# LSH attention and a feed-forward block on one core: all 192 normalisations on POOL, and a schedule that holds the durations of a trace

## The chip, the core and the metric

The kernel runs on one core of a Trainium2 chip. A core has five engines with queues of their own: PE (TensorE, matrix products and transposes), DVE (VectorE), ACT (ScalarE), POOL (GpSimd) and SP (SyncE, which here only issues transfers). Each works through its instructions in the order in which they were written and waits on semaphores. The metric is the device time of one launch in microseconds.

## The reference

Attention in which a query sees only the keys of its own hash bucket, and a two-layer feed-forward block on what it gives. Batch 4, 8 heads, 768 rows, head size 64; model width 512, inner width 2048; float32, but for the two weight matrices, which come as doubles.

```python
q_bucket = sum(((q @ proj) > 0) * powers)          # 6 bits; k_bucket likewise
scores = where(q_bucket == k_bucket, (q @ k.T) / 8, -1e9)
scores = scores - max(scores); attn = exp(scores)
attn = attn / (sum(attn) + 1e-9)
x = (attn @ v)                                     # heads side by side: 3072 x 512
h = x @ w_in
out = (s * relu(h)**2 + b) @ w_out
```

A query whose bucket holds no key keeps the score -1e9 in every column, and its weights are all 1/768.

## The kernel before

The work is cut into 96 slots: a slot is 256 queries of one head of one batch (two tiles of 128 queries). In each slot:

- `weights(i, a, pr)`, once for each tile a: two groups of score products of 384 keys (L416 for batch 0, in float32; L418 and L419 afterwards, in split float32r), the row maximum on DVE (L426), the exponential with its row sum on ACT (L427), and on DVE four one-column instructions, `inverse` (L433 to L436), that give the row's factor `rz` and summand `u`. The last of the four, L436, multiplies a comparison of one column with another column. Then the tile is normalised in place: e times rz plus u. For the second tile (a = 1) that is one DVE instruction right behind the inverse (L440), for the first tile (a = 0) one POOL instruction of the same form (L444).
- `values(i, pr, pieces)`: the normalised tiles are transposed by PE (L470, four at a time, two of each tile, so each set needs both tiles), copied out of PSUM (L475, or L481 with the rest L482) and multiplied with the values (L489, or L491 and L492); the result goes to `xpb`, is split into a high and a low part (L508, L509) and written out.
- Between the slots `prep` splits q and k of a later head, hashes them and copies their parts together (L344 to L369); `decode` turns one of 32 weight tiles from doubles into two float32r parts, with ACT (L287, L288, L293), DVE (L289, L290) and POOL (L291, L299, for half of them L298); `moe` is the feed-forward block of 256 rows in eight steps (L545 to L547 into the inner layer, ACT L551 to L553 and POOL L554, L562 to L564 out of it), 96 steps in all.

The score banks 0 and 1 of PSUM are shared by all tiles (for the first seven slots, 6 and 7 too): the next tile's scores can be written only when the exponential has read them.

Nothing is issued in the order in which it is written. Each piece is put on a `Plan` with an engine, a cost in microseconds, the keys that it reads and writes, and a priority. `Plan.order` is a list scheduler: it runs the pieces against these costs (and `HOP`, what a result takes to another engine) and gives each engine's queue its order. No time of the plan reaches the chip, only the order. The costs come from the helpers `act`, `dve` and `pool`, as a slope and a constant or as a number at the place of the call:

```python
def act(n, fn, r, w, pr, more=0.0):
    plan.add(ACT, 0.095 + n / 1200.0 + more, fn, r, w, pr)
```

Weights of a slot have the priority 10 i - 8, values 10 i + 5, decoding 10 i + 15, steps of `moe` from 100000 on: they fill.

Of the kernel before, what the change touches and what calls it, by code (L numbers as in the profile page):

```python
# [14 lines left out]
AF = mybir.ActivationFunctionType  # L15
ALU = mybir.AluOpType
# [11 lines left out]
PE, DVE, ACT, POOL, SP = (mybir.EngineType.PE, mybir.EngineType.DVE, mybir.EngineType.Activation,  # L28
                          mybir.EngineType.Pool, mybir.EngineType.SP)
# [80 lines left out]
def lsh_attention_moe(ctx: ExitStack, tc, q, k, v, proj, w_in, w_out, s, b, out):  # L110
    nc = tc.nc
    B, H, S, D = q.shape
# [4 lines left out]
    HS = S // 2  # L117
    CH = 256
# [15 lines left out]
    plan = Plan()  # L134

    def f32(ap):
        return ap.bitcast(F32)

    def tile_(name, shape, dt=F32):
        return const.tile(shape, dt, name=name)  # L140
# [5 lines left out]
    def pe(cost, fn, r, w, pr):  # L146
        plan.add(PE, cost, fn, r, w, pr)

    def dve(n, fn, r, w, pr, ns=None):
        plan.add(DVE, ((n + 64) / 960.0 if ns is None else ns), fn, r, w, pr)  # L150

    def act(n, fn, r, w, pr, more=0.0):
        plan.add(ACT, 0.095 + n / 1200.0 + more, fn, r, w, pr)

    def pool(n, fn, r, w, pr, ns=None):
        plan.add(POOL, (0.15 + n / 430.0 if ns is None else ns), fn, r, w, pr)
# [29 lines left out]
    xsb = tile_("xsb", [P, 2, CH], F32R)  # L186
# [6 lines left out]
    st = tile_("st", [P, NST, 4])  # L193
    thr, big, s_sb, b_sb, qk_sb = [misc[:, x:x + 1] for x in range(5)]
# [114 lines left out]
    def AK(x, r=(0, 1), g=(0, 1)):  # L309
        return [("aq", x, i, j) for i in r for j in g]  # L310

    def BK(x, r=(0, 1), g=(0, 1)):
        return [("bq", x, i, j) for i in r for j in g]
# [18 lines left out]
    def prep(w, i, pr):  # L332

        x, y, h, exact = visits[w]["x"], w % 2, visits[w]["h"], w < EARLY
        aq, bq, ks, nat = EQ[h] if exact else AQ[y], BQ[y], KS[y], NAT[y]
        mk, NK = nat.rearrange("p t j d -> p (t j d)"), [("nat", y, 0), ("nat", y, 1)]

        def split(g, i, pr):
            pb = fill_bank(i)
            cols, o = slice(g * HS, (g + 1) * HS), bank[:, pb, 0:HS]  # L340

            def tr():
                for t in range(HT):
                    nc.tensor.transpose(out=bank[:, pb, t * P:(t + 1) * P], in_=nat[:, g * HT + t], identity=ident)  # L344
            pe(0.33, tr, NK, [("b", pb)], pr)
            act(HS, lambda: nc.scalar.activation(aq[:, cols], o, AF.Copy, scale=qk_sb), [("b", pb)], AK(x, g=(g,)), pr)
            if exact:
                if g:
                    dma(lambda: EK[h][0:D, 0:S], lambda: aq[D:P, 0:S], AK(x, r=(1,)), [("ks", x, 0)], pr, D * S * 4)
                return  # L350
            dve(HS, lambda: nc.vector.scalar_tensor_tensor(bq[:, cols], o, qk_sb, f32(aq[:, cols]), ALU.mult, ALU.subtract), [("b", pb)] + AK(x, g=(g,)), BK(x, g=(g,)), pr, 0.55)
            if g:
                dma(lambda: ks[0:D], lambda: aq[D:P].rearrange("p (o n) -> p o n", o=1).broadcast_to([D, 2, S]), AK(x, r=(1,)), [("ks", x, 0)], pr, 2 * D * S * 4)
                dma(lambda: ks[D:P, 0], lambda: bq[D:P], BK(x, r=(1,)), [("ks", x, 1)], pr, D * S * 4)

        def hash_(g, i, pr):
            pb = fill_bank(i)
            cols, o = slice(g * HS, (g + 1) * HS), bank[:, pb, 0:HS]

            def mm():  # L360
                if exact:
                    nc.tensor.matmul(o[0:D], pj, aq[:, cols], start=True, stop=True)
                    return
                nc.tensor.matmul(o[0:D], pjh, aq[:, cols], start=True, stop=False)
                nc.tensor.matmul(o[0:D], pjl, aq[:, cols], start=False, stop=False)
                nc.tensor.matmul(o[0:D], pjh, bq[:, cols], start=False, stop=True)
            pe(mmc(HS, 4 if exact else 3), mm, AK(x, g=(g,)) + ([] if exact else BK(x, g=(g,))), [("b", pb)], pr)

            dve(HS, lambda: nc.vector.tensor_scalar(mk[0:KB + MR, cols], o[0:KB + MR], thr[0:KB + MR], big[0:KB + MR], ALU.is_gt, ALU.mult),  # L369
                [("b", pb)], NK, pr, 0.67)  # L370
            if g and exact:
                dma(lambda: EK[h][D:HR, 0:S], lambda: mk[KB:KB + MR], NK, [("ks", x, 2)], pr, MR * S * 4)
                dma(lambda: aq[D:HR, 0:S], lambda: mk[0:MR], NK, AK(x, r=(1,)), pr, MR * S * 4)
            elif g:
                dma(lambda: aq[D:P], lambda: aq[0:D], AK(x, r=(0,)), AK(x, r=(1,)), pr, D * S * 4)
                dma(lambda: ks[D:HR, 1], lambda: mk[KB:KB + MR], NK, [("ks", x, 2)], pr, MR * S * 4)
                dma(lambda: bq[D:HR], lambda: mk[0:MR], NK, BK(x, r=(1,)), pr, MR * S * 4)
            if g:
                n = preps.index(w) + 2
                if n < len(preps):  # L380
                    load(preps[n], pr)
        return [lambda i, pr, f=f, g=g: f(g, i, pr) for f in (split, hash_) for g in range(2)]
# [20 lines left out]
    def weights(i, a, pr):  # L403

        bb, h, c, w = slots[i]
        x, t, j, exact = visits[w]["x"], c * TPC + a, TPC * i + a, bb == 0
        b0 = 6 if i < EARLY - 1 and j % 2 else 0
        bk = [("b", b0), ("b", b0 + 1)]
        aq, bq, ks = AQ[w % 2], BQ[w % 2], KS[w % 2]
        ts = slice(t * P, (t + 1) * P)  # L410

        for g in range(2):
            def mm(g=g):
                cols, o = slice(g * HS, (g + 1) * HS), bank[:, b0 + g, 0:HS]
                if exact:
                    nc.tensor.matmul(o, EQ[h][0:HR, ts], EK[h][0:HR, cols], start=True, stop=True)  # L416
                    return
                nc.tensor.matmul(o, aq[:, ts], ks[:, 0, cols], start=True, stop=False)  # L418
                nc.tensor.matmul(o, bq[0:HR, ts], ks[0:HR, 1, cols], start=False, stop=True)  # L419
            pe(mmc(HS, 4 if exact else 2), mm, AK(x) + KK(x) + ([] if exact else BK(x)), [bk[g]], pr)  # L420
        y = j % NST
        nm, z, rz, u = [st[:, y, m:m + 1] for m in range(4)]
        e, ek = eb[:, j % NE], ("e", j % NE)

        sc = bank[:, b0:b0 + 2, 0:HS]
        dve(S, lambda: nc.vector.tensor_reduce(nm, sc, AX.XY, ALU.max, negate=True), bk, [("st", y, 0)], pr, 0.95)  # L426
        act(S, lambda: nc.scalar.activation(e.rearrange("p (g n) -> p g n", g=2), sc, AF.Exp, bias=nm, accum_out=z),  # L427
            bk + [("st", y, 0)], [ek, ("st", y, 1)], pr, 0.45)

        def inverse():
            nc.vector.tensor_scalar(rz, z, EPS, None, ALU.add)  # L433
            nc.vector.tensor_scalar(u, nm, -FLOOR, 1.0 / (S + EPS), ALU.is_gt, ALU.mult)
            nc.vector.reciprocal(rz, rz)
            nc.vector.scalar_tensor_tensor(rz, nm, -FLOOR, rz, ALU.is_le, ALU.mult)  # L436
        if a or i < DV:
            def norm():
                inverse()
                nc.vector.tensor_scalar(e, e, rz, u, ALU.mult, ALU.add)  # L440
            dve(S, norm, [("st", y, 0), ("st", y, 1)], [ek, ("st", y, 2)], pr, 1.37)
        else:
            dve(1, inverse, [("st", y, 0), ("st", y, 1)], [("st", y, 2)], pr, 0.65)
            pool(S, lambda: nc.gpsimd.tensor_scalar(e, e, rz, u, ALU.mult, ALU.add), [("st", y, 2)], [ek], pr, 2.23)  # L444

    xp, xd = {}, {}
    nx = [0]
# [1 line left out]
    def values(i, pr, pieces):  # L449


        bb, h, c, w = slots[i]

        vs, exact = VS[w % 2], i < EARLY
        x = visits[w]["x"] if exact else w % 2
# [5 lines left out]
        for f in range(HT):  # L461
            tb, y = fill_bank(i), nfill[1] % NPH
# [37 lines left out]
        t, tk = xp[key]  # L500
        xh, xk = t[hh * D:(hh + 1) * D], [tk + (hh,)]
# [3 lines left out]
        if hh:  # L505

            xk = [tk + (0,), tk + (1,)]
            act(CH, lambda: nc.scalar.copy(xsb[:, 0, :], t), xk, [("xs", 0)], pr)  # L508
            dve(CH, lambda: nc.vector.tensor_tensor(xsb[:, 1, :], t, f32(xsb[:, 0, :]), ALU.subtract), xk + [("xs", 0)], [("xs", 1)], pr)  # L509
            xd[key] = tc.dram_tile([P, 2, CH], F32R, name=f"xd{key[0]}_{key[1]}_{key[2]}")  # L510
            dma(lambda: xd[key], lambda: xsb, [("xs", 0), ("xs", 1)], [("xd", key)], pr, 262144)

# [77 lines left out]
    for i in range(NSL):  # L590
        pr = 10.0 * i
        bb, h, c, w = slots[i]
# [29 lines left out]
FIRST = 2.0  # L622
RATE = 1.6
PACE = 4
DV = 0
WP = -8
MP = 0.0
PP = 0
# [26 lines left out]
```

## Time and profile before

| what | value |
|---|---|
| median of 3 runs | 1154.06 us (1150.02 to 1154.14) |
| profiled execution, its own time | 1155.39 us |
| its span, first to last instruction | 1153.6 us |
| mean granted clock of TensorE | 0.964 |
| normalisations on DVE (L440) | 96, mean 815 ns |
| normalisations on POOL (L444) | 96, mean 1009 ns |

A line such as "L440 DVE TENSOR_SCALAR eb<-eb,st 128x768 ... x96" is a group: source line, engine, operation, what is written from what, shape, count. Behind the bar stand the busy time in us, the mean of one in ns, and the idle time of the engine just before these instructions with what ended it. A wait "PE bank L470 <- DVE eb L440: 11.2, 11, 2.5" reads: PE's instruction of L470 waited for DVE's of L440, 11.2 us in total, 11 times, the longest 2.5 us. The clock is the share of full speed that TensorE was granted.

### The profile page before, as it was taken

The numbers are of one execution on the slowest core, as the hardware profiler recorded it, in microseconds if no ns is written. First come the engines' busy times: TensorE is split into PE (matmuls) and PEld (weight loads), VectorE is DVE, ScalarE is ACT, GpSimd is POOL, SyncE is SP. The second block draws the span as 40 slices with busy tenths as digits, with TensorE's granted clock in tenths as the row PEclk, the third lists the DMA queues.
The fourth block names the chain that finished last, engine by engine and source line by source line (L and its number), as shares of the span: only waits on it lengthen the run. The fifth ranks groups of instructions, "written<-read, shape, count | busy, mean of one in ns | idle before, by whom it ended". The sixth has DMA issues, their size and how long they took to land.

```text
span 1153.6 us, 18828 instructions
## 1 busy us (share of the span) xinstructions
PE 1093.0 (95%) x6898; PEld 956.9 (83%) x6898; DVE 730.2 (63%) x1682; ACT 649.3 (56%) x1297; POOL 361.6 (31%) x318
## 2 busy tenths in 40 slices
PE   5987799988799999999999999999999999999998
PEld 2444487766699999989999999999999999999997
DVE  2666779868787878777777788778788860000000
ACT  2655476746566665756656666666666553333332
POOL 1465546635332222222222222222222222222221
PEclk7888899969899999999999999999999999999999
DMA  7463121213423342243243224324233201011010
GB/s 187 140 181 105 49 69 48 100 46 101 124 62 87 72 127 61 70 120 80 58 114 88 60 79 121 81 51 134 65 79 83 68 24 60 7 49 56 1 37 19
DMA packets 87980, 91.14 MB, mean 79 GB/s; under 512 B 55888, under 2 KB 61008, under 8 KB 87888
## 3 DMA queue, kind: packets, MB, share of 16 engines
q1 hardware_dynamic: 82976, 73.16, 23.7%
q10 hardware_dynamic: 4912, 16.78, 4.8%
q8 instruction: 54, 0.88, 0.3%
q14 instruction: 38, 0.31, 0.1%
HBM read 48.24 MB, written 18.87 MB: 58 GB/s over the span
## 4 chain that ended last, share of the span: by engine, by line
PE 86%; DVE 7%; DMA 2%; ACT 2%; issue 2%; SPq 0%; POOLq 0%; ACTq 0%; DVEq 0%
PE bank L470 10%; PE bank L545 8%; PE bank L546 8%; PE bank L547 8%; PE bank L564 7%; PE bank L563 7%; PE bank L562 7%; PE bank L492 5%; PE bank L491 5%; PE bank L416 5%; PE bank L419 4%; PE bank L418 4%; PE bank L489 2%; PE bank L344 2%; DVE eb L440 1%
## 5 line engine op out<-in xcount | busy, mean ns | idle before, releaser
L481 ACT CAST phdt.float32r<-bank 128x512 fp32r<-128x512 f32 x264 | 153.3, 585 | 177.0 <-PE bank L470 157.0
L426 DVE TENSOR_REDUCE st<-bank 128x1 f32<-128x768 f32 x192 | 183.3, 955 | 78.5 <-PE bank L416 39.6
L545 PE MATMUL bank<-xc,w 128*128 128x256 f32 x768 | 227.6, 296 | 0.0
L554 POOL TENSOR_TENSOR glb<-rb,ghb 128x512 fp32r<-128x512 f32 x96 | 124.8, 1300 | 317.1 <-ACT ghb L553 227.8
L546 PE MATMUL bank<-xc,w 128*128 128x256 f32 x768 | 217.9, 284 | 1.1 <-POOL w L299 1.1
L547 PE MATMUL bank<-xc,w 128*128 128x256 f32 x768 | 217.7, 283 | 0.0
L427 ACT ACTIVATE eb<-bank,st 128x768 f32<-128x768 f32 x192 | 173.6, 904 | 67.3 <-DVE st L426 66.1
L482 DVE TENSOR_TENSOR plb<-bank,phdt.float32r 128x512 fp32r<-128x512 f32 x264 | 178.4, 685 | 45.9 <-ACT phdt.float32r L481 44.2
L444 POOL TENSOR_SCALAR eb<-eb,st 128x768 f32<-128x768 f32 x96 | 96.9, 1009 | 334.7 <-DVE st L436 144.6
L470 PE MATMUL bank<-ident,eb 128*128 128x128 f32 x1152 | 180.0, 282 | 15.0 <-DVE eb L440 14.3
L470 PEld LDWEIGHTS bank<-ident,eb 128*128 128x128 f32 x1152 | 140.5, 145 | 37.7 <-DVE eb L440 16.3
L562 PE MATMUL bank<-w,ghb 128*128 128x512 f32 x384 | 156.9, 409 | 0.0
L564 PE MATMUL bank<-w,glb 128*128 128x512 f32 x384 | 152.2, 396 | 0.2 <-POOL glb L554 0.2
L563 PE MATMUL bank<-w,ghb 128*128 128x512 f32 x384 | 151.5, 395 | 0.0
L546 PEld LDWEIGHTS bank<-xc,w 128*128 128x128 f32 x768 | 147.1, 192 | 5.1 <-POOL w L299 1.6
L545 PEld LDWEIGHTS bank<-xc,w 128*128 128x128 f32 x768 | 147.0, 191 | 4.8 <-issue 0.7
L491 PE MATMUL bank<-phdt.float32r,vs 128*128 128x256 f32 x528 | 149.0, 304 | 1.6 <-ACT phdt.float32r L481 1.6
L547 PEld LDWEIGHTS bank<-xc,w 128*128 128x128 f32 x768 | 147.0, 191 | 0.0
L492 PE MATMUL bank<-plb,vs 128*128 128x256 f32 x528 | 139.8, 287 | 2.0 <-DVE plb L482 1.5
L551 ACT ACTIVATE rb<-bank 128x512 f32<-128x512 f32 x96 | 57.4, 598 | 147.7 <-PE bank L547 147.2
L570 DVE SCALAR_TENSOR_TENSOR osb<-bank,misc,bcs 128x512 f32<-128x512 f32 x24 | 17.4, 746 | 193.4 <-PE bank L564 193.2
L492 PEld LDWEIGHTS bank<-plb,vs 128*128 128x128 f32 x528 | 101.4, 192 | 9.9 <-DVE plb L482 4.3
(77 smaller groups left out, 1832.9 us busy)
## 6 DMA issues: line engine op xcount, KB each, us to landing
xd<-xsb SPq DMA_DIRECT2D x48, 256.0 KB
xc<-xd SPq DMA_DIRECT2D x48, 256.0 KB
ks<-aq SPq DMA_DIRECT2D x24, 384.0 KB
raw<-in_moe_w_in_dram ACTq DMA_DIRECT2D x16, 512.0 KB
raw<-in_moe_w_out_dram ACTq DMA_DIRECT2D x16, 512.0 KB
nat<-in_q_dram SPq DMA_DIRECT2D x32, 192.0 KB
nat<-in_k_dram SPq DMA_DIRECT2D x32, 192.0 KB
out_dram<-osb SPq DMA_DIRECT2D x24, 256.0 KB
```

The lines of the kernel that those rows point to most:

```text
L426: dve(S, lambda: nc.vector.tensor_reduce(nm, sc, AX.XY, ALU.max, negate=True), bk, [("st", y, 0)], pr, 0.95)
L427: act(S, lambda: nc.scalar.activation(e.rearrange("p (g n) -> p g n", g=2), sc, AF.Exp, bias=nm, accum_out=z), bk + [("st", y, 0)], [ek, ( ...
L470: nc.tensor.transpose(out=bank[:, tb, o:o + P], in_=eb[:, es[a], kt * P:(kt + 1) * P], identity=ident)
L482: dve(512, lambda ph=ph, pl=pl, src=src: nc.vector.tensor_tensor(pl, src, f32(ph()), ALU.subtract), [("b", tb), ("ph", y)], [("pl", y)], p ...
L491: nc.tensor.matmul(av, vs[:, kt], PH[0][:, y, m], start=(kt == 0), stop=False)
L492: nc.tensor.matmul(av, vs[:, kt], plb[:, y, m], start=False, stop=(kt == NT - 1))
L545: nc.tensor.matmul(hp, w[:, 0, fs], xc[:, 0, :], start=(cc == 0), stop=False)
L546: nc.tensor.matmul(hp, w[:, 1, fs], xc[:, 0, :], start=False, stop=False)
L547: nc.tensor.matmul(hp, w[:, 0, fs], xc[:, 1, :], start=False, stop=(cc == NC_ - 1))
L562: nc.tensor.matmul(o, gh[:, ts], w[:, 0], start=(f == 0), stop=False)
L563: nc.tensor.matmul(o, gh[:, ts], w[:, 1], start=False, stop=False)
L564: nc.tensor.matmul(o, gl[:, ts], w[:, 0], start=False, stop=(f == NF - 1))
```

## The change

Both tiles of a slot are normalised on POOL; DVE does the inverse alone. The constant `DV`, which was 0, goes. And costs of the plan are replaced: POOL's normalisation 1.01 us (2.23), the inverse 0.70 (0.65 alone, 1.37 together with DVE's normalisation), ACT's slope 1050 elements a microsecond (1200), the constant of the exponential 0.28 (0.45), of the scaled copy in `prep` 0.12 (none), its rest on DVE 0.61 (0.55), and the low part of x 0.5 (the slope gave 0.33).

```diff
     def act(n, fn, r, w, pr, more=0.0):
-        plan.add(ACT, 0.095 + n / 1200.0 + more, fn, r, w, pr)
+        plan.add(ACT, 0.095 + n / 1050.0 + more, fn, r, w, pr)
...
-            act(HS, lambda: nc.scalar.activation(aq[:, cols], o, AF.Copy, scale=qk_sb), [("b", pb)], AK(x, g=(g,)), pr)
+            act(HS, lambda: nc.scalar.activation(aq[:, cols], o, AF.Copy, scale=qk_sb), [("b", pb)], AK(x, g=(g,)), pr, 0.12)
...
         act(S, lambda: nc.scalar.activation(e.rearrange("p (g n) -> p g n", g=2), sc, AF.Exp, bias=nm, accum_out=z),
-            bk + [("st", y, 0)], [ek, ("st", y, 1)], pr, 0.45)
+            bk + [("st", y, 0)], [ek, ("st", y, 1)], pr, 0.28)
...
-        if a or i < DV:
-            def norm():
-                inverse()
-                nc.vector.tensor_scalar(e, e, rz, u, ALU.mult, ALU.add)
-            dve(S, norm, [("st", y, 0), ("st", y, 1)], [ek, ("st", y, 2)], pr, 1.37)
-        else:
-            dve(1, inverse, [("st", y, 0), ("st", y, 1)], [("st", y, 2)], pr, 0.65)
-            pool(S, lambda: nc.gpsimd.tensor_scalar(e, e, rz, u, ALU.mult, ALU.add), [("st", y, 2)], [ek], pr, 2.23)
+        dve(1, inverse, [("st", y, 0), ("st", y, 1)], [("st", y, 2)], pr, 0.70)
+        pool(S, lambda: nc.gpsimd.tensor_scalar(e, e, rz, u, ALU.mult, ALU.add), [("st", y, 2)], [ek], pr, 1.01)
...
-            dve(CH, lambda: nc.vector.tensor_tensor(xsb[:, 1, :], t, f32(xsb[:, 0, :]), ALU.subtract), xk + [("xs", 0)], [("xs", 1)], pr)
+            dve(CH, lambda: nc.vector.tensor_tensor(xsb[:, 1, :], t, f32(xsb[:, 0, :]), ALU.subtract), xk + [("xs", 0)], [("xs", 1)], pr, 0.5)
```

The text is six lines shorter behind the edit: L444 is L438 in the changed kernel, L470 is L464, L545 is L539, L554 is L548; up to L436 the numbers stay.

In the order, POOL's queue around the decoding of the fifteenth weight tile (raw_200 is that tile as it was read, w_... the tile decoded, bcs the column sums). Before:

```order
L444 TENSOR_SCALAR eb<-eb,st 128x768
L299 TENSOR_TENSOR w_809<-osb,w_809 128x512
L291 TENSOR_TENSOR osb<-osb,raw_200 128x512
L298 TENSOR_TENSOR bcs<-bcs,osb 128x512
L299 TENSOR_TENSOR w_846<-osb,w_846 128x512
L444 TENSOR_SCALAR eb<-eb,st 128x768
```

and now:

```order
L438 TENSOR_SCALAR eb<-eb,st 128x768
L299 TENSOR_TENSOR w_808<-osb,w_808 128x512
L291 TENSOR_TENSOR osb<-osb,raw_200 128x512
L438 TENSOR_SCALAR eb<-eb,st 128x768
L299 TENSOR_TENSOR w_834<-osb,w_834 128x512
```

A second normalisation stands between L291 and L299 of this tile, and the sum L298 has moved behind them.

The same place on DVE, which makes raw_200's bits (L289, L290) and then the inverse of a second tile. Before:

```order
L290 SCALAR_TENSOR_TENSOR osb<-osb,raw_200 128x512
L433 TENSOR_SCALAR st<-st 128x1
L434 TENSOR_SCALAR st<-st 128x1
L435 RECIPROCAL st<-st 128x1
L436 SCALAR_TENSOR_TENSOR st<-st 128x1
L440 TENSOR_SCALAR eb<-eb,st 128x768
L426 TENSOR_REDUCE st<-bank 128x1
```

and now:

```order
L290 SCALAR_TENSOR_TENSOR osb<-osb,raw_200 128x512
L433 TENSOR_SCALAR st<-st 128x1
L434 TENSOR_SCALAR st<-st 128x1
L435 RECIPROCAL st<-st 128x1
L436 SCALAR_TENSOR_TENSOR st<-st 128x1
L289 TENSOR_SCALAR raw_201<-osb 128x512
L426 TENSOR_REDUCE st<-bank 128x1
```

The normalisation is gone, and a part of the next tile's decoding stands in its place ahead of the next maximum.

More of the change, by code (lines that the diff above doesn't have):

```diff
@@ L350, in split @@
                 return
-            dve(HS, lambda: nc.vector.scalar_tensor_tensor(bq[:, cols], o, qk_sb, f32(aq[:, cols]), ALU.mult, ALU.subtract), [("b", pb)] + AK(x, g=(g,)), BK(x, g=(g,)), pr, 0.55)
+            dve(HS, lambda: nc.vector.scalar_tensor_tensor(bq[:, cols], o, qk_sb, f32(aq[:, cols]), ALU.mult, ALU.subtract), [("b", pb)] + AK(x, g=(g,)), BK(x, g=(g,)), pr, 0.61)
             if g:
@@ L624 @@
 PACE = 4
-DV = 0
 WP = -8
```

## The prediction

> **What bounds the kernel now.** I read the page first (shares and the 40 slices), then the busy times by stage, then what TensorE waited for in each stage, then the groups, the chain and the timeline of the one stage in which it waits.
>
> ```profile
> span 1153.6 us, 18828 instructions
> ...
> PE 1093.0 (95%) x6898; PEld 956.9 (83%) x6898; DVE 730.2 (63%) x1682; ACT 649.3 (56%) x1297; POOL 361.6 (31%) x318
> ...
> PE   5987799988799999999999999999999999999998
> ...
> DVE  2666779868787878777777788778788860000000
> ...
> PEclk7888899969899999999999999999999999999999
> ```
>
> TensorE (PE) is busy for 95% of the span, and the slices say where the other 5% lies: in the first eleven of the forty. The same stretch has the lowered clock. The busy times of four stretches make that exact (columns: stretch, its length, then PE, weight load, DVE, ACT and POOL busy with their counts, PE's granted clock, DMA share, GB/s):
>
> ```profile
> 0.00:120.00 120.00, 92.89 (x319) 50.12 (x319) 66.18 (x153) 61.10 (x119) 53.43 (x51) 0.83 0.56 149
> 120.00:325.00 205.00, 176.98 (x948) 140.49 (x947) 164.81 (x334) 125.18 (x258) 104.11 (x90) 0.90 0.25 76
> 325.00:925.00 600.00, 598.71 (x4199) 562.76 (x4198) 476.10 (x1148) 383.50 (x789) 153.03 (x138) 1.00 0.32 84
> 925.00:1153.60 228.60, 224.46 (x1438) 203.51 (x1436) 23.09 (x47) 79.55 (x135) 50.99 (x40) 1.00 0.09 32
> ```
>
> PE is idle for 27.1 us, 28.0 us, 1.3 us and 4.1 us of them. From 325 us on it is full at clock 1.00, so what DVE or POOL do there is hidden as long as they deliver in time. Only the first 325 us can get shorter. What PE waited for there, first 0 to 120 us, then 120 to 325 us (total, times, longest):
>
> ```profile
> PE bank L416 <- DMA eq<-in_v_dram: 7.2, 1, 7.2
> PE bank L344 <- DMA nat<-in_k_dram: 7.1, 2, 5.5
> PE bank L416 <- DMA eq<-nat: 3.3, 1, 3.3
> ```
>
> ```profile
> PE bank L470 <- DVE eb L440: 11.2, 11, 2.5
> PE bank L416 <- ACT eb L427: 8.2, 6, 1.7
> PE bank L364 <- DVE nat L369: 1.6, 1, 1.6
> ```
>
> The first 120 us wait on transfers, 17.6 us in these three rows, which the change does not touch. In the second stretch PE waits for two things: 11 times for the normalisation of a slot's second tile (L440, on DVE), and 6 times for an exponential (L427) to give back the score banks. The change moves the first; the second hangs on DVE's maximum (L426). The groups of that stretch (count, then busy us, mean ns, idle before):
>
> ```profile
> L440 DVE TENSOR_SCALAR eb<-eb,st 128x768 f32<-128x768 f32 x19 | 20.7, 1090 | 0.7
> L444 POOL TENSOR_SCALAR eb<-eb,st 128x768 f32<-128x768 f32 x20 | 20.7, 1034 | 56.7 <-DVE st L436 39.9 <-PE bank L470 10.8 <-PE bank L547 5.8
> L436 DVE SCALAR_TENSOR_TENSOR st<-st 128x1 f32<-128x1 f32 x38 | 18.7, 491 | 1.3
> L291 POOL TENSOR_TENSOR osb<-osb,raw 128x512 int32<-128x512 int32 x18 | 23.3, 1293 | 24.4 <-ACT eb L427 9.8 <-PE bank L492 4.2 <-DVE st L433 3.5
> ```
>
> The same normalisation takes 1.09 us on DVE and 1.03 us on POOL here. A timeline piece shows why DVE is so slow (start, duration, engine, line):
>
> ```profile
> 118.27 0.15 DVE L433 TENSOR_SCALAR st<-st 128x1 f32<-128x1 f32 x1 [1.13 <-ACT eb L427]
> 118.51 1.28 POOL L298 TENSOR_TENSOR bcs<-bcs,osb 128x512 f32<-128x512 f32 x1
> 118.65 1.15 DVE L436 SCALAR_TENSOR_TENSOR st<-st 128x1 f32<-128x1 f32 x1
> 119.98 0.98 POOL L444 TENSOR_SCALAR eb<-eb,st 128x768 f32<-128x768 f32 x1 [0.19 <-DVE st L436]
> ...
> 122.29 1.56 PE L416 MATMUL bank<-ek,eq 76*128 76x384 f32 x4 [1.72 <-ACT eb L427]
> 123.33 1.28 POOL L291 TENSOR_TENSOR osb<-osb,raw 128x512 int32<-128x512 int32 x1 [1.15 <-ACT osb L287]
> 123.50 1.13 DVE L436 SCALAR_TENSOR_TENSOR st<-st 128x1 f32<-128x1 f32 x1
> 124.67 1.70 DVE L440 TENSOR_SCALAR eb<-eb,st 128x768 f32<-128x768 f32 x1
> 124.69 1.26 POOL L298 TENSOR_TENSOR bcs<-bcs,osb 128x512 f32<-128x512 f32 x1
> 126.29 0.94 DVE L426 TENSOR_REDUCE st<-bank 128x1 f32<-128x768 f32 x1
> 126.42 1.33 PE L470 MATMUL bank<-ident,eb 128*128 128x128 f32 x5 [2.47 <-DVE eb L440]
> ```
>
> L436 works on one element per partition, yet it ends when POOL's instruction ends: 119.80 against 119.79 us, then 124.63 against 124.61 us. L440, behind it, is held by the next one (L298 to 125.95) and ends at 126.37. So one slot pays twice: PE stands 2.47 us, and the next maximum, whose scores were ready at 123.85 (122.29 + 1.56), starts 2.44 us late.
>
> **The change part by part.** All 96 of L440 leave DVE, 20.7 of its 164.8 busy us in the stretch that counts. POOL gets 19 more there; at 0.98 us it goes from 104.1 to 122.7 busy of 205 us (51% to 60%). The sum is of PE's idle time in that stretch.
>
> (a) Maxima no longer wait behind L440. What this is worth is the row of exponentials late for PE: between 0 and -8.2 us. The piece above has 1.70 of 2.44 us in L440, near the full end; in the new order a part of the decoding (L289) stands between L436 and the maximum at that place, which keeps some of it. I take -6.
>
> (b) The path from the inverse (end of L436) to PE's transposes. Before: 0.04 + 1.09 + 0.05 = 1.18 us (gaps from 124.63 to 124.67 and 126.37 to 126.42). After: 0.18 (119.80 to 119.98) + 0.98 + POOL to PE. The last gap I take from POOL's other client:
>
> ```profile
> 261.50 1.26 POOL L299 TENSOR_TENSOR w<-osb,w 128x512 fp32r<-128x512 f32 x1
> 262.82 0.39 PE L546 MATMUL bank<-xc,w 128*128 128x256 f32 x1 [1.12 <-POOL w L299]
> ```
>
> 0.06 us, so 1.22 us if POOL is free: +0.04 in each of 11 waits, +0.4 us in all. If each time a decoding instruction of 1.29 us goes first, 2.51 us: +14.6 us. In POOL's new order the normalisation stands right behind the L291 whose end releases L436, so it can start at once at that place; I take a fifth of the way, +3.
>
> (c) L436 meets POOL more often: its excess is 18.7 - 38 x 0.16 = 12.6 us; with POOL at 60% instead of 51% it is 14.9, +2.3 on DVE. The chain of that stretch holds it at 5.8% of 205 us, 11.9 of its 18.7 us, so about two thirds count: +1.5 (ends 0 and +2.3).
>
> ```profile
> by line: PE bank L416 14.1%; PE bank L470 10.1%; issue 5.9%; DVE st L436 5.8%; DVE eb L440 5.6%; PE bank L492 5.2%; DVE osb L290 5.0%; DVE st L426 4.2%; PE bank L491 3.9%; DVE plb L482 3.8%; ACT eb L427 3.1%; ACT phdt.float32r L481 2.6%; DM
> ```
>
> (d) L290, DVE's part of a weight's decoding, is 5.0% of the chain, 10.3 us, since the inverse queues behind it. With 20.7 of 164.8 us (13%) off the queue it comes earlier; I take a quarter, -2.5 (ends 0 and -4).
>
> (e) The cost table (ACT's slope, the exponential, L351 and L509) does no work of its own; it moves the order. MoE steps placed ahead of the 24th slot are 7.8 before and 7.9 after, the last slot has 59.6 and 60.6 of 96 ahead of it, so PE's work before and after 325 us is the same: 0. SP's queue has 360 rows in both; two pairs of loads (q and k of the sixth and the eighth head) go behind one or two copies. PE's waits for such loads are in the first stretch, 7.1 us in 2; I take 0, ends -3 and +3.
>
> Sum of idle: -6 + 3 + 1.5 - 2.5 = -4 us. The clock adds to that: at 0.90 the 177 us of work in the stretch are 17.7 us longer than at 1.00, beside 28 us of idle, 0.63 us for each idle us. That makes -6.5 us. The profiled execution took 1155.4 us (1.8 around the span), 1.3 above the median of the runs: 1148.9 against it, 1147.5 against the median.
>
> What hides the rest: from 325 us on POOL goes from 153 to 219 of 600 us (67 x 0.98 more), and 67 slots now hand their second tile to POOL. The cover is that PE has other work there. The plan allows 0.70 + 0.13 + 1.01 + 0.10 = 1.94 us from the inverse's start to the transposes; the rows give 0.54 (118.27 to the start of L436, and 0.16) + 0.18 + 0.98 + 0.06 = 1.76. If that cover goes, the rival below has its price.
>
> ```profile
> L436 DVE SCALAR_TENSOR_TENSOR st<-st 128x1 f32<-128x1 f32 x135 | 22.3, 165 | 4.6
> L444 POOL TENSOR_SCALAR eb<-eb,st 128x768 f32<-128x768 f32 x67 | 67.4, 1005 | 238.7 <-DVE st L436 77.1 <-PE bank L492 54.2 <-ACT aq L346 28.1
> ```
>
> These are L436 and POOL's normalisation from 325 to 925 us. L436 runs at 165 ns though POOL is busy a quarter of the time: POOL starts its long instructions right behind L436 or behind an ACT result, and the next L436 comes only after another exponential.
>
> **The rivals.** *POOL's queue makes it slower.* POOL works in order and carries the decoding. If the normalisation waits w behind it in each of the 11 cases, the idle changes by 11 x (0.04 + w) - 6 + 1.5 - 2.5; it breaks even at w = 0.60 us, and at a whole L291 (1.29) it is +7.6, with the clock +12.4: 1166.5 us. For: POOL is busy 60% of the stretch. Against: the held L436 means that POOL comes free at that very moment. Chance 0.15.
>
> *The relief changes nothing.* The bank loop (scores, maximum, exponential) goes on without the normalisation, and (a) and (d) are taken up by other DVE work that stood behind L440; then (b) and (c) cancel what is left: 1154 us. For: ACT's L427 waits are 6, L440's 11. Chance 0.25.
>
> *The full stretch loses its cover.* If L436 is held there as it is before 325 us, by (491 - 160) ns at a POOL share of 51%, then at the new share of 36% it is about 0.24 us late, and if PE waits for it in each of 67 slots, that is +16 us: 1163.5 us. Against: the 165 ns above, and PE's 1.3 us of idle in 600. Chance 0.08. The Trainium skill (GPSIMD Engine Reference, 1. Specifications) says that GpSimd shares its SBUF interfaces with VectorE and lists as contention VectorE's instructions with two SBUF inputs or in a 2-port mode. By that rule alone L436, which reads two SBUF columns, would be held wherever POOL works, and 1163.5 us would be the forecast; the trace bears it out at 491 ns up to 325 us and not at 165 ns after.
>
> *The change does not do what it says:* ruled out; no DVE instruction of that shape is left in the new order, and POOL has 192.
>
> **How the numbers follow.** The gain of some microseconds is likeliest: 1147.5 us, its own range 1139 to 1153 (from (a) at its end with (b) at +0.4, to half of (a)), chance 0.52. Half a per cent is 5.8 us, about what a measurement can tell from no change (the three runs spread over 4.1 us): below 1148.3 is faster. Of the 0.52, 0.45 lies below that and 0.07 above. Faster 0.45, the same 0.07 + 0.25 = 0.32, slower 0.15 + 0.08 = 0.23. The range leaves out the slower part of the slower cases, and below it reaches most of the way to (a) and (d) at their ends with the clock (-8.2 + 0.4 + 1.5 - 4 = -10.3, times 1.63: 1137.3): 1137 to 1161.
>
> **What would show it.** Right: in 120 to 325 us PE's idle falls from 28 to about 24 us and the clock rises a little; waits of L416 for L427 fall to 2 or 3 us; PE waits for L438 on POOL some 11 to 14 us in all; L436 rises to 0.55 us there and stays near 0.17 after; 325 to 925 us stays under 5 us idle. Wrong: PE's waits for POOL over 20 us, decoding ahead of L438 on POOL, L436 above 0.3 us after 325 us, or a change in the first 120 us, where the order moves but no row prices it.

## The result, and the profile after

The changed kernel takes 1160.86 us (median of 9 runs, 1156.63 to 1165.70) against 1152.28 us (9 runs, 1149.79 to 1155.22) for the kernel before on the same chip: a ratio of 1.0074, 95% interval 1.0052 to 1.0096. It is slower by 0.7%, where faster by 0.6% was forecast. The profiled execution took 1156.63 us, the shortest of its nine, while the profiled execution of before (1155.39 us) lay above the longest of its nine: the two traces stand closer to each other than the medians. The page of the changed kernel (span, engines, the slices of PE and its clock):

```profile
span 1154.8 us, 19001 instructions
...
PE 1090.9 (94%) x6898; PEld 954.7 (83%) x6898; DVE 659.6 (57%) x1586; ACT 650.0 (56%) x1297; POOL 453.8 (39%) x414
...
PE   5877799978899999989999999999999999999998
...
PEclk7789899988799999999999999999999999999999
```

The work has moved as planned: DVE 730.2 to 659.6 us, POOL 361.6 to 453.8. PE's weak slices are still the first eleven. The same stretches as before (length, then PE, weight load, DVE, ACT, POOL busy with counts, granted clock, DMA share, GB/s):

```profile
0.00:120.00 120.00, 85.51 (x281) 45.17 (x281) 59.77 (x138) 57.13 (x110) 53.29 (x52) 0.83 0.51 141
120.00:325.00 205.00, 184.61 (x1008) 145.81 (x1009) 151.89 (x330) 130.74 (x270) 130.59 (x116) 0.92 0.26 81
325.00:925.00 600.00, 595.04 (x4159) 558.44 (x4158) 420.68 (x1060) 379.62 (x778) 216.12 (x204) 1.00 0.32 84
```

From 120 to 325 us PE's idle time falls from 28.0 to 20.4 us, more than the 4 us forecast. But the first 120 us go from 27.1 to 34.5 idle, and hold 281 of PE's instructions instead of 319: the program is behind when the stretch ends. And 325 to 925 us go from 1.3 to 5.0. A stretch that ends at a fixed time mixes a delay with what it displaces, so from here on the stretches end at events of the trace: the start at the first maximum of the eighth slot, decoding where PE multiplies the finished column sums of the weights (L304, 8 to 12 us behind the last weight tile). Before, then after, the start and the decoding stretch:

```profile
0.00:116.20 116.20, 89.09 (x301) 47.66 (x302) 63.74 (x149) 58.27 (x113) 49.91 (x48) 0.82 0.58 154
116.20:328.60 212.40, 184.38 (x991) 146.39 (x991) 170.31 (x347) 129.95 (x267) 107.64 (x93) 0.90 0.24 74
```

```profile
0.00:124.80 124.80, 89.41 (x301) 47.55 (x302) 63.14 (x141) 58.91 (x113) 58.01 (x55) 0.84 0.51 141
124.80:326.00 201.20, 181.71 (x999) 144.42 (x999) 148.94 (x327) 129.95 (x268) 125.87 (x113) 0.92 0.25 79
```

The same 301 instructions of PE fill the start. It is 8.6 us longer, with 35.4 us of idle instead of 27.1: +8.3. The decoding stretch is 11.2 us shorter, with 19.5 instead of 28.0: -8.5. The two cancel, and what is lost in the full stretch (+3.7) stays.

What PE waited for in the start, the two rows that grew most (before, then after; "issue" is idle time for which the view finds no releaser):

```profile
PE bank L344 <- DMA nat<-in_k_dram: 7.1, 2, 5.5
PE bank L416 <- issue: 2.4, 1, 2.4
```

```profile
PE bank L344 <- DMA nat<-in_k_dram: 9.3, 3, 5.1
PE bank L416 <- issue: 9.2, 4, 3.5
```

Most of the +8.3 us is the second row, waits of score products (L416). The four begin 3.7 to 5.9 us after the issue of their own head's last copy, so that copy is likely what they wait for.

What PE waited for in the changed kernel, 120 to 325 us (total, times, longest):

```profile
PE bank L486 <- DVE plb L476: 6.8, 10, 1.4
PE bank L464 <- POOL eb L438: 6.4, 4, 2.9
PE bank L416 <- ACT eb L427: 3.0, 3, 1.7
PE bank L418 <- ACT eb L427: 2.5, 2, 1.4
```

and from 325 to 925 us:

```profile
PE bank L486 <- DVE plb L476: 3.0, 5, 1.2
PE bank L344 <- DVE bq L351: 1.2, 1, 1.2
PE bank L464 <- POOL eb L438: 0.3, 1, 0.3
```

The normalisation on POOL stops PE 4 times for 6.4 us (on DVE it was 11 times, 11.2 us). The banks cost 5.5 us (8.2). New is the wait of the value products for the low part of the copied tiles (L476 on DVE, behind ACT's copy L475): 6.8 us against 1.5, and 3.0 of the 5.0 us that PE idles in the full stretch.

### The profile page after: what moved, and what is told of

The parts are those of the page before. It is cut to its first block, busy times and chain, and to the rows that moved or that the text cites. A ratio compares the mean times of both kernels' runs of the same rounds, so it can differ in the third digit from the quotient of the medians.

```text
span 1154.8 us, 19001 instructions
## 1 busy us (share of the span) xinstructions
PE 1090.9 (94%) x6898; PEld 954.7 (83%) x6898; DVE 659.6 (57%) x1586; ACT 650.0 (56%) x1297; POOL 453.8 (39%) x414
## 4 chain that ended last, share of the span: by engine, by line
PE 86%; DVE 5%; DMA 4%; issue 2%; ACT 1%; POOL 1%; SPq 0%; POOLq 0%; ACTq 0%; DVEq 0%
PE bank L464 9%; PE bank L539 8%; PE bank L540 8%; PE bank L541 8%; PE bank L558 7%; PE bank L556 7%; PE bank L557 7%; PE bank L486 5%; PE bank L416 5%; PE bank L485 5%; PE bank L419 4%; PE bank L418 4%; PE bank L483 2%; PE bank L344 2%; DMA eq<-nat 1%
## 5 line engine op out<-in xcount | busy, mean ns | idle before, releaser
L438 POOL TENSOR_SCALAR eb<-eb,st 128x768 f32<-128x768 f32 x192 | 191.3, 997 | 416.4 <-DVE st L436 340.9
L539 PE MATMUL bank<-xc,w 128*128 128x256 f32 x768 | 228.5, 298 | 0.2 <-ACT rb L545 0.2
L475 ACT CAST phdt.float32r<-bank 128x512 fp32r<-128x512 f32 x264 | 152.4, 583 | 126.6 <-PE bank L464 107.8
L476 DVE TENSOR_TENSOR plb<-bank,phdt.float32r 128x512 fp32r<-128x512 f32 x264 | 179.3, 686 | 60.2 <-ACT phdt.float32r L475 59.1
L548 POOL TENSOR_TENSOR glb<-rb,ghb 128x512 fp32r<-128x512 f32 x96 | 124.3, 1295 | 224.7 <-ACT ghb L547 186.3
L464 PE MATMUL bank<-ident,eb 128*128 128x128 f32 x1152 | 169.8, 276 | 7.1 <-POOL eb L438 7.0
L464 PEld LDWEIGHTS bank<-ident,eb 128*128 128x128 f32 x1152 | 135.2, 142 | 22.9 <-POOL eb L438 10.6
L539 PEld LDWEIGHTS bank<-xc,w 128*128 128x128 f32 x768 | 147.3, 192 | 5.8 <-ACT rb L545 0.7
L486 PE MATMUL bank<-plb,vs 128*128 128x256 f32 x528 | 140.7, 288 | 9.8 <-DVE plb L476 9.8
L485 PE MATMUL bank<-phdt.float32r,vs 128*128 128x256 f32 x528 | 146.2, 298 | 1.7 <-ACT phdt.float32r L475 1.7
L545 ACT ACTIVATE rb<-bank 128x512 f32<-128x512 f32 x96 | 57.3, 597 | 147.9 <-PE bank L541 147.7
L564 DVE SCALAR_TENSOR_TENSOR osb<-bank,misc,bcs 128x512 f32<-128x512 f32 x24 | 17.5, 749 | 188.4 <-PE bank L558 188.3
L486 PEld LDWEIGHTS bank<-plb,vs 128*128 128x128 f32 x528 | 101.0, 191 | 19.5 <-DVE plb L476 14.3
```

The source lines that it names most:

```text
L464: nc.tensor.transpose(out=bank[:, tb, o:o + P], in_=eb[:, es[a], kt * P:(kt + 1) * P], identity=ident)
L476: dve(512, lambda ph=ph, pl=pl, src=src: nc.vector.tensor_tensor(pl, src, f32(ph()), ALU.subtract), [("b", tb), ("ph", y)], [("pl", y)], p ...
L485: nc.tensor.matmul(av, vs[:, kt], PH[0][:, y, m], start=(kt == 0), stop=False)
L486: nc.tensor.matmul(av, vs[:, kt], plb[:, y, m], start=False, stop=(kt == NT - 1))
L539: nc.tensor.matmul(hp, w[:, 0, fs], xc[:, 0, :], start=(cc == 0), stop=False)
```

## The experiments

The main theory (A in the expectations below): the new order of the start, in which the copies of the later heads go out later, costs more than the decoding stretch gains. Against it stand that the cost table does it, that POOL's greater load does it, and that L436, held by POOL, does it.

All runs with their own kernel before on the same chip. Start and decoding are the two stretches just defined, full the one up to 925 us. "Idle" is length minus PE busy. "Clock" is (1 - granted clock) times PE busy, the time that the lowered clock added; the rows have the clock in two digits, so it is good to half a microsecond in the start and one in decoding. In hash_ahead, copy_time and both_mends some 15 of PE's 301 instructions of the start fall behind its end, so there the two stretches are best read together. The last column is the profiled execution's own time.

| kernel | median, us | ratio to before | start: length, idle, clock | decoding: length, idle, clock | full: idle | profiled |
|---|---|---|---|---|---|---|
| before | 1152.28 | | 116.2, 27.1, 16.0 | 212.4, 28.0, 18.4 | 1.3 | 1155.39 |
| after | 1160.86 | 1.0074 (1.0052 to 1.0096) | 124.8, 35.4, 14.3 | 201.2, 19.5, 14.5 | 5.0 | 1156.63 |
| after_again | 1162.50 | 1.0057 (1.0032 to 1.0081) | 133.2, 33.7, 24.9 | 204.8, 19.2, 18.6 | 5.0 | 1168.84 |
| old_start | 1140.60 | 0.9885 (0.9839 to 0.9931) | 112.9, 26.5, 13.0 | 191.9, 19.2, 6.9 | 5.0 | 1135.32 |
| new_start | 1161.70 | 1.0067 (1.0036 to 1.0097) | 130.9, 32.9, 22.5 | 203.1, 27.5, 8.8 | 1.3 | 1161.20 |
| norms_only | 1148.61 | 0.9957 (0.9924 to 0.9989) | 112.4, 30.1, 10.7 | 202.3, 19.9, 12.8 | 5.7 | 1143.75 |
| costs_only | 1149.50 | 0.9971 (0.9938 to 1.0003) | 111.6, 24.8, 13.0 | 205.7, 28.4, 7.1 | 4.2 | 1146.12 |
| hash_ahead | 1138.18 | 0.9837 (0.9808 to 0.9867) | 111.9, 25.8, 16.4 | 192.7, 18.1, 3.5 | 5.0 | 1135.31 |
| copy_time | 1143.18 | 0.9902 (0.9867 to 0.9937) | 112.1, 27.3, 16.1 | 195.1, 17.5, 8.9 | 6.1 | 1142.63 |
| no_hold | 1157.63 | 1.0011 (0.9987 to 1.0034) | 128.0, 34.7, 17.7 | 198.2, 19.0, 12.5 | 5.0 | 1157.15 |
| old_start_no_hold | 1134.45 | 0.9807 (0.9779 to 0.9834) | 115.9, 27.3, 16.0 | 186.8, 17.3, 3.4 | 5.0 | 1133.44 |
| both_mends | 1133.97 | 0.9820 (0.9784 to 0.9857) | 108.8, 24.0, 14.4 | 193.4, 16.1, 7.1 | 5.0 | 1132.84 |

The kernels before of the three batches had 1153.33 us (29 runs: old_start, new_start, norms_only, costs_only), 1155.09 us (23 runs: hash_ahead, after_again and the two no_hold) and 1156.46 us (12 runs: both_mends, copy_time).

### The start as before, the rest as after

The first eight slots (the eight heads of batch 0) are normalised and costed as before, the other 88 as after.

```diff
+    new_ = [False]
-        plan.add(ACT, 0.095 + n / 1050.0 + more, fn, r, w, pr)
+        plan.add(ACT, 0.095 + n / (1050.0 if new_[0] else 1200.0) + more, fn, r, w, pr)
...
+        if new_[0]:   # as after: inverse on DVE, normalisation on POOL; else as before
...
+        new_[0] = i >= EARLY   # EARLY is 8; set ahead of each slot
```

> The first eight slots, with the preparation and decoding planned in them, are normalised and costed as before; from the ninth slot on everything is as in the changed kernel. Theory A (the loss sits in the order of the first eight slots, where scores that wait for a copy now stand ahead of the hash that starts the next head's copies; behind it the change gains): the first 120 us as before, idle of PE from 120 to 325 us about 20 us instead of 28, time 1143 to 1148 us, ratio to before 0.992 to 0.996. Rival B (the loss is spread, the one profiled run hides it): 1155 to 1160 us. Rival C (late shifts in the full stretch): idle there over 5 us, 1155 us or more.

It is 1140.60 us, ratio 0.9885. Its two stretches:

```profile
0.00:112.90 112.90, 86.45 (x304) 46.34 (x305) 64.39 (x149) 58.06 (x113) 50.09 (x48) 0.85 0.58 156
112.90:304.80 191.90, 172.68 (x994) 137.83 (x993) 147.19 (x329) 130.54 (x269) 128.22 (x113) 0.96 0.27 83
```

The start has before's idle time (26.5 us) and the decoding stretch after's (19.2). What the change does past the eighth slot is a gain. All of the loss, and more, comes from how eight slots of 96 are planned.

### The start as after, the rest as before

```diff
-        new_[0] = i >= EARLY
+        new_[0] = i < EARLY
```

> The reverse: the first eight slots are normalised and costed as in the changed kernel, everything from the ninth on as before. Theory A: about 10 us lost in the first 125 us, nothing gained behind, 1160 to 1165 us, ratio 1.007 to 1.011. Rivals B and C: within 3 us of before.

It is 1161.70 us, ratio 1.0067: the loss of the whole change with the change in the first eight slots alone.

```profile
0.00:130.90 130.90, 97.98 (x301) 52.02 (x302) 62.54 (x142) 58.69 (x113) 59.69 (x56) 0.77 0.50 137
130.90:334.00 203.10, 175.62 (x991) 139.32 (x992) 165.27 (x346) 130.10 (x267) 106.06 (x93) 0.95 0.25 77
```

The start idles 32.9 us, decoding 27.5 as before. The full stretch has 1.3: its 3.7 us come from the slots that follow.

### The normalisations alone, and the cost table alone

Norms_only normalises as after with its two costs (0.70 and 1.01) and leaves every other cost as it was. Costs_only is the reverse: the normalisation split over DVE and POOL at the old 1.37, 0.65 and 2.23, the other costs new.

```diff
 norms_only, against after
-    plan.add(ACT, 0.095 + n / 1050.0 + more, fn, r, w, pr)
+    plan.add(ACT, 0.095 + n / 1200.0 + more, fn, r, w, pr)
...  (likewise 0.12, 0.61, 0.28 and 0.5 back to none, 0.55, 0.45 and none)
```

> All 192 normalisations on POOL with their new costs (0.70 and 1.01), all other costs of the plan as before. In the order the scores of the third head stand ahead of the second hash half of the fourth, as in the changed kernel. Theory A: time as the changed kernel, 1156 to 1164 us. Rival D (the other costs, ACT's slope above all, shifted the order): 1145 to 1150 us.

> The other costs as in the changed kernel (ACT's slope, exponential, scaled copy, its rest, low part of x), the normalisations split between DVE and POOL as before with the costs of before. In the order the hash of the fourth and the sixth head stands ahead of the scores, as before. Theory A: 1150 to 1155 us, as before. Rival D: 1157 to 1163 us.

Norms_only, expected by A to be about as slow as after, gave 1148.61 us (0.9957): a miss. Costs_only gave 1149.50 us (0.9971, the interval reaches 1.0003), so the cost table alone isn't it either. The stretches, norms_only first, then costs_only:

```profile
0.00:112.40 112.40, 82.31 (x301) 44.79 (x302) 64.27 (x143) 61.36 (x117) 66.86 (x60) 0.87 0.59 159
112.40:314.70 202.30, 182.37 (x1022) 146.10 (x1022) 147.08 (x325) 129.38 (x267) 121.50 (x108) 0.93 0.25 77
```

```profile
0.00:111.60 111.60, 86.80 (x301) 46.82 (x302) 62.80 (x144) 56.22 (x109) 44.91 (x44) 0.85 0.59 156
111.60:317.30 205.70, 177.26 (x1005) 140.56 (x1006) 176.72 (x357) 136.52 (x277) 112.12 (x98) 0.96 0.25 79
```

Decoding's idle time goes with the normalisations (19.9 with all on POOL, 28.4 with the split). The long start goes with neither: 112.4 and 111.6 us. It takes both together, so "the normalisations on POOL are bad for the start" and "the new durations are bad" both fall. The waits of the score products in the start follow the loss: for transfers or without a named releaser, L416 waits 19 to 20 us in after, after_again, new_start and no_hold, and 8 to 13 us in the other eight kernels of the table. What comes late there is seen in the timeline.

### Which instruction is late in the start

PE and SP's queue around the third slot, before (start, duration, engine, line, counts). L362 is one half of a head's hash, L416 x8 are the scores of the third slot, L144 issues a head's copies:

```profile
43.38 0.86 PE L362 MATMUL bank<-eq,pj 128*64 128x384 f32 x2
...
45.68 0.81 PE L362 MATMUL bank<-eq,pj 128*64 128x384 f32 x2
46.41 2.85 PE L416 MATMUL bank<-ek,eq 76*128 76x384 f32 x8
...
47.22 0.80 SPq L144 DMA_DIRECT2D ek<-nat  x1
...
108.81 0.79 SPq L144 DMA_DIRECT2D ek<-nat  x1
```

and after:

```profile
40.95 0.86 PE L362 MATMUL bank<-eq,pj 128*64 128x384 f32 x2
...
42.10 0.76 SPq L144 DMA_DIRECT2D eq<-nat  x1
...
47.24 4.73 PE L416 MATMUL bank<-ek,eq 76*128 76x384 f32 x8 [2.92 <-DMA eq<-nat]
...
55.10 0.81 PE L362 MATMUL bank<-eq,pj 128*64 128x384 f32 x2
56.64 0.80 SPq L144 DMA_DIRECT2D ek<-nat  x1
...
118.45 0.80 SPq L144 DMA_DIRECT2D ek<-nat  x1
```

Before, the fourth head's second hash half (45.68) is ahead of the third slot's scores (46.41), and its copy leaves at 47.22 us. After, the scores have gone ahead of it. They need the third head's copy, issued at 42.10, and start at 47.24, 5.1 us later. The plan gives such a copy 0.7 + 1.8 + 0.14 = 2.64 us (the issue, the hop and its 36 KB by the plan's rate), so for the plan the scores were ready and, having the higher priority, came first. The hash half, which needs nothing more, waits in PE's queue behind them until 55.10, and its copy leaves at 56.64, 9.4 us later than before. From there both kernels take the same 61.6 to 61.8 us to the eighth head's copy (108.81 and 118.45): the delay is not made up. The same step comes back with every head: its scores wait for its copy, and the next head's hash half stands behind these scores. In the code the second hash half also issues the load of the head after next (`load(preps[n], pr)`), so a late hash makes the next heads late in turn. Norms_only has the scores ahead as well, at this place and at the later heads, but there the third head's copies had gone out 2.4 us earlier and its scores ran without a wait at full clock (2.82 us), so its fourth head's copy leaves at 50.24 and its eighth's at 102.89. So this order of hash and scores does not cost time by itself; it costs where the scores have to wait for the copy. What in the rest of the order makes them wait in after and not in norms_only was not isolated.

### The hash put ahead by one edge

The smallest edit against that: a key that only the plan knows makes the third slot's scores wait for the fourth head's hash. No instruction changes, only the order, though the plan carries a moved piece on to all that is planned behind it.

```diff
-            pe(..., mm, AK(x, g=(g,)) + ..., [("b", pb)], pr)                       # hash, L362
+            pe(..., mm, AK(x, g=(g,)) + ..., [("b", pb)] + ([("hashed", w)] if exact and g else []), pr)
...
-            pe(..., mm, AK(x) + KK(x) + ..., [bk[g]], pr)                           # scores, L416
+            pe(..., mm, AK(x) + KK(x) + ... + ([("hashed", w + 1)] if i == 2 else []), [bk[g]], pr)
```

> The changed kernel with one order turned round, nothing else: the scores of the third head (slot 2) are planned behind the second hash half of the fourth head. Costs, engines and instructions are those of the changed kernel. Theory A, made sharper (in the first 125 us one displacement costs the time: the fourth head's hash waits on PE behind scores that wait for the third head's copy, so its own copies leave at 56.6 instead of 47.2 us, and all later heads follow at the same 15.4 us each): the eighth head's copies leave at 105 to 110 us instead of 118.5, time 1140 to 1150 us, 8 to 15 below the changed kernel. Rival E (the start is late for another reason, such as the order of the loads or less work for POOL and DVE to lean on): within 3 us of the changed kernel.

It is 1138.18 us, ratio 0.9837; after_again, the changed kernel itself on the same chip, had 1162.50.

> The changed kernel itself, for a second profile. Both theories: 1157 to 1165 us; idle of PE in its first 125 us about 35 us, from there to the end of the decoding 19 to 20 us, in the full stretch 4 to 6 us; the loss by the lowered clock differs from profile to profile by some us.

The order that this one edge makes is worth 24.3 us. The timeline (the last PE rows are the sixth head's second hash half and the fifth slot's scores) and the stretches of hash_ahead:

```profile
47.60 0.81 PE L362 MATMUL bank<-eq,pj 128*64 128x384 f32 x2
48.34 2.85 PE L416 MATMUL bank<-ek,eq 76*128 76x384 f32 x8
...
49.53 0.85 SPq L144 DMA_DIRECT2D ek<-nat  x1
...
76.14 0.81 PE L362 MATMUL bank<-eq,pj 128*64 128x384 f32 x2
76.88 2.85 PE L416 MATMUL bank<-ek,eq 76*128 76x384 f32 x8
...
104.49 0.80 SPq L144 DMA_DIRECT2D ek<-nat  x1
```

```profile
0.00:111.90 111.90, 86.14 (x285) 46.12 (x285) 60.97 (x138) 57.19 (x109) 54.64 (x53) 0.81 0.56 153
111.90:304.60 192.70, 174.64 (x1011) 137.39 (x1011) 151.02 (x330) 132.86 (x273) 130.87 (x116) 0.98 0.27 85
```

The fourth head's copy leaves at 49.53 and the eighth's at 104.49, 14 us earlier than after. Half of that (7.1 us) is there at the fourth head; the other half comes behind it, since the edge changes the order of later heads too: the sixth head's second hash half now runs ahead of the fifth slot's scores (76.14 and 76.88), where in after it came behind them (88.93 and 80.08), and the copies of the later heads go out two by two (72.26 and 78.04, 99.39 and 104.49). So the run shows what the order is worth, not what the one pair is worth. The idle time of both stretches falls by 11.0 us against after's profile (54.9 to 43.9). The clock gives another 8.9 (28.8 to 19.9), all of it in decoding. Against after_again's profile it is 9.0 and 23.6. The clocks of all runs on that chip say the same: the median is 0.9725 in hash_ahead and 0.9605 in after_again, and within the changed kernel a hundredth of clock goes with 8 us (last section), which makes some 10 us, an estimate. So about 10 us of the 24.3 are idle time and about as much is clock, whose share differs from execution to execution.

### The copy's time in the plan

If the plan's 1.8 us for a transfer is what puts the scores ahead, the measured time should mend it without an edge. The chip's instructions are after's; only the hop is changed.

```diff
-HOP = {None: 0.0, PE: 0.2, DVE: 0.13, ACT: 0.2, POOL: 0.1, SP: 1.8}
+HOP = {None: 0.0, PE: 0.2, DVE: 0.13, ACT: 0.2, POOL: 0.1, SP: 4.6}
```

> The changed kernel with one more cost of the plan taken from the trace: a copy's result takes 4.6 instead of 1.8 us to reach its reader (the piece of the chain from issue to the scores that waited was 5.5 us, planned were 2.6). In the order every hash then stands ahead of the scores that wait for a copy. Theory A, one step further back (the order of the start is wrong because the plan thinks that copies land early): the eighth head's copies leave before 112 us, 1138 to 1150 us. Rival H (the longer copies push other work apart, or the order of the start was wrong for another reason): 1155 us or more.

It is 1143.18 us, ratio 0.9902. The hash is ahead of the scores again:

```profile
45.63 0.81 PE L362 MATMUL bank<-eq,pj 128*64 128x384 f32 x2
...
47.23 2.85 PE L416 MATMUL bank<-ek,eq 76*128 76x384 f32 x8
47.53 0.74 SPq L144 DMA_DIRECT2D ek<-nat  x1
```

The start idles 27.3 us, as before. It does not reach hash_ahead: past 925 us PE idles 7.1 us instead of 4.1, and in the full stretch 6.1 instead of 5.0. The hop counts for all transfers and moves other places too, which would explain it; no run tells that apart.

### L436 without its second tensor

L436 reads two columns of SBUF as tensors. The factor can be given as a scalar operand of a `tensor_scalar` instead, with the same result.

```diff
-            nc.vector.scalar_tensor_tensor(rz, nm, -FLOOR, rz, ALU.is_le, ALU.mult)
+            nc.vector.tensor_scalar(rz, nm, -FLOOR, rz, ALU.is_le, ALU.mult)
```

> The changed kernel with L436 in another form: a tensor_scalar with rz as a column operand in place of a scalar_tensor_tensor that reads two tensors; order and results as in the changed kernel. Theory F (L436 is held until POOL's running instruction ends because it reads two tensors from SBUF): its mean in 120 to 325 us falls from 470 to about 160 ns, DVE's busy time there by 12 us, and PE's idle by 3 to 6 us: 1152 to 1158 us. Rival G (any DVE instruction on these columns is held, or the hold lies off PE's path): mean unchanged, or time within 3 us of the changed kernel.

> The kernel old_start (first eight slots normalised and costed as before, the rest as in the change) with the same other form of L436. Theory F: 2 to 6 us below old_start's 1140.6, ratio to before 0.984 to 0.988. Rival G: the same as old_start, 0.9885.

> The changed kernel with the hash of the fourth head ahead of the third head's scores and L436 as a tensor_scalar. If the two act in different stretches they add: hash_ahead's 1138 less 3 to 6 us, 1132 to 1136 us, ratio 0.979 to 0.982. If the held L436 was already covered once the start is mended: 1137 to 1140 us.

The groups of L436 in the changed kernel, 120 to 325 us, then 325 to 925 us (count, busy us, mean ns):

```profile
L436 DVE SCALAR_TENSOR_TENSOR st<-st 128x1 f32<-128x1 f32 x40 | 18.8, 470 | 1.4
```

```profile
L436 DVE SCALAR_TENSOR_TENSOR st<-st 128x1 f32<-128x1 f32 x132 | 23.3, 176 | 4.5
```

and in no_hold:

```profile
L436 DVE TENSOR_SCALAR st<-st 128x1 f32<-128x1 f32 x40 | 8.6, 214 | 1.4
```

```profile
L436 DVE TENSOR_SCALAR st<-st 128x1 f32<-128x1 f32 x132 | 28.3, 214 | 4.6
```

In this form it takes 214 ns in both stretches, whatever POOL does: the hold is gone, at a price of 38 ns where there was none. For this line, then, it is the form with two tensors that is held. The Trainium skill (GPSIMD Engine Reference, 1. Specifications) lists VectorE's instructions with two SBUF inputs among those that contend with GpSimd. The trace agrees: 470 ns with two, 214 with one. It does not follow that a `tensor_scalar` is never held: L440 is one, over 768 columns, and took 1.70 us beside L298 in the rows of the prediction. In time the new form is worth little: 1157.63 us against after_again's 1162.50 on the same chip, -4.9 us, ratio 1.0011 against 1.0057; the intervals just overlap. With the start mended it gives -4.2 us (both_mends against hash_ahead) and -6.2 us (old_start_no_hold against old_start), from different batches each; by the ratios, each to its own kernel before, it is about 2 and 9 us. All three point the same way, and 4 to 6 us is the likeliest size. It did not make the change slower, since the kernel before has the same hold (491 ns). Both_mends, at 1133.97 us, and old_start_no_hold, at 1134.45, are the fastest: 0.982 and 0.981 of the kernel before, both with all the later normalisations on POOL.

## Why the prediction was wrong

The forecast was 1147.5 us with 0.45 for faster; the result lies at the upper end of the range. The step that failed is **(e)**, the moves of the order. It had taken 0 with ends of -3 and +3 from two facts, that the steps of the feed-forward block ahead of the 24th slot are as many, and that SP's queue has as many rows. Neither says anything of the first 120 us, where one hash half went behind scores that wait for a transfer. There the prediction had written that PE waits on transfers "which the change does not touch"; the change moved the issue of these transfers, the fourth head's copy from 47.22 to 56.64 us. Measured: +8.3 us of idle in the start by the first profile, +6.6 by the second, and the clock beside it. The text had named a change there as what would make it wrong, "where the order moves but no row prices it". A row did price it: the wait of L416 for `eq<-nat`, 3.3 us in one go in the waits of before, said what happens to whatever stands behind such a score group in PE's queue. The question what had been put behind a wait was asked of POOL and DVE, and not of PE.

The other steps, against 120 to 325 us or, where said, the decoding stretch:

- **(a)** maxima no longer behind the normalisation, -6: the waits for the exponential fell from 8.2 to 5.5 us, so -2.7. In the changed kernel they are 3.0 for L416 alone, as forecast, but 2.5 us more had moved to L418.
- **(b)** from the inverse to PE, +3: wrong in sign. The waits for the normalisation went from 11.2 (11 times) to 6.4 us (4 times), -4.8. That POOL comes free when L436 ends, as the prediction argued, fits this.
- **(c)** L436 meets POOL more, +1.5, with 0.55 us each: 470 ns, less than the 491 before. So 0, though POOL's share rose from 51% to 64%: the mean does not follow POOL's share.
- **(d)** decoding's L290 earlier, -2.5: no wait of PE shows it, and no run tells it apart.
- Not in the sum: the wait for the low part of the copied tiles (L486 for L476), +5.3 us. With normalised tiles coming earlier, the copies out of PSUM are what PE waits for next.
- The sum of the stretch was -4; between the events its idle fell by 8.5, from 28.0 to 19.5. Norms_only (19.9) and old_start (19.2) have the same fall, costs_only (28.4) and new_start (27.5) do not: it comes from the normalisations on POOL past the eighth slot. The gain in idle time was there, twice as large as forecast, and was given back ahead of it.
- **The cover in the full stretch** went from 1.3 to 5.0 us of idle, at the edge of "under 5 us". It went neither by L436 (176 ns) nor by POOL (0.3 us): 3.0 us of it is L486 waiting for L476 again, 1.2 us L344 waiting for L351. The rival of 16 us is refuted, and its mechanism with it.
- **The clock**, 0.63 us for each idle us, did not hold. Before and costs_only idle 55.1 and 53.2 us in the two stretches, and lose 34.4 and 20.1 us to the clock. The two profiles of the same changed kernel lose 28.8 and 43.5.

In sum: idle +8.3 - 8.5 + 3.7 = +3.5 us by the first profile (33.7 + 19.2 + 5.0 against 56.4, +1.5, by the second), where the medians differ by 7 to 9 us. Part of the rest is clock: on the chip of after_again the median clock of the runs was 0.9605, against 0.965 of the 23 runs of before, and at 8 us for a hundredth that is some 4 us, an estimate. The split isn't settled beyond that, because a profile shows one execution and the clock differs between executions by more.

That the plan of the first eight slots is the cause is shown by old_start and new_start, which take it out or put it in alone, and that it is their order, and not POOL's work there, by hash_ahead, which has the same instructions on the same engines. Which displacement within the start does it is argued from the timeline: the hash half behind the waiting scores is the first, but hash_ahead moves later heads too, and norms_only has the same pair in the same order without the loss. Why a better order of the start gains as much clock as idle time, and gains it in decoding (14.5 to 3.5 us in hash_ahead), stays open.

## What to carry to other kernels

When a list schedule's costs change, look at each in-order queue for the first place where something that needs nothing now stands behind something that waits for a transfer, above all at the start, where each head feeds the next. Measure transfers from issue to reader and put that into the plan along with the compute times: corrected costs for the engines beside a transfer time of about half the measured one (2.64 against 5.1 us) gave a worse order than the old ones, and with a longer hop (copy_time) a better one. And test a change of order by halves of the program (these slots old, the rest new): that told in two runs that a change measured as a loss was a gain of 1 to 2% with one stretch to mend.

## What the runs showed of the hardware

Eight score products of the same shape took 2.85 us (46.41 in before) and, in the changed kernel, 4.73 us and this:

```profile
80.08 5.46 PE L416 MATMUL bank<-ek,eq 76*128 76x384 f32 x8 [3.54 <-issue]
```

The last is 1.92 times the first, behind 3.54 us of idle. The Trainium skill (TensorE: Matmul & The Clock Gate, Part 1) has two clock states, half and full, set by the activity of windows of about 3.4 us that run freely. The factor of 1.92 agrees with the two states; no run here shows the windows. What was not expected is how much of the lowered clock comes and goes with the program unchanged. The second profile of the changed kernel, start and decoding:

```profile
0.00:133.20 133.20, 99.53 (x301) 52.41 (x301) 61.16 (x141) 58.79 (x113) 60.93 (x57) 0.75 0.49 134
133.20:338.00 204.80, 185.60 (x998) 147.08 (x998) 148.39 (x327) 129.98 (x268) 123.07 (x110) 0.90 0.24 77
```

The same instructions with 0.75 instead of 0.84 in the start: 8.4 us more there, with 1.7 us less idle. Over its nine runs the kernel's mean clock went from 0.956 at 1165.70 us to 0.967 at 1156.63, about 8 us for each hundredth.

One element per partition can cost more than a microsecond (L436, 1.15 us in the row of before) when POOL's long instruction runs beside it, and for this line the form decides: 470 ns in the mean as `scalar_tensor_tensor`, 214 as `tensor_scalar` in the same place.
